# Wider parameter products, merged transposing loads, a dropped plane and moved stores in a backward pass of a state-space and SwiGLU block

## The chip, the cores and the metric

One NeuronCore of one Trainium2 chip runs the whole program in one launch. TensorE does the matrix products, VectorE and ScalarE the elementwise work, GpSimd a little elementwise work and one of the transfer queues; SyncE only issues transfers. SyncE, ScalarE and GpSimd each work through their own transfers in order, and an issue that must wait holds up what stands behind it on that engine. The metric is the device time of the launch in microseconds (us).

## What is computed

The forward pass, and then the gradients of its output with respect to twelve of its inputs. `L` is 2048 rows, `D` 576 channels, `N` 128 states per channel, `F` 4608 hidden units; everything comes in and goes out as bf16.

```python
xn  = layernorm(x)                                   # x is A_u
dt  = exp(log_dt);  A = A_re + 1j*A_im               # [D, N]
K   = einsum("dn,dnl,dn->dl", C, exp(dt*A*l), dt*B).real
s   = causal_conv(K, xn) + xn*Dskip                  # by FFT, length 2L
g   = silu((silu(xn @ w1) * (xn @ w3)) @ w2)
out = x + s*g
# returned: out and d<out, grad_out> / d(A_u, A_re, A_im, B_re, B_im, C_re, C_im,
#                                        log_dt, Dskip, w1, w3, w2)
```

So the backward pass needs, beside the gradients of the weights, the sum over the 2048 positions of the gradient of `K` against `exp(dt*A*l)`, for each channel and state, with and without a factor `l`: these sums are the "parameter sums" `S_all` below. With `l = a*64 + b` the exponential is split into a table over `b` (called Q, 64 values) and one over `a` (called P or PZ, `AV` = 32 values), each with a real and an imaginary plane.

## The kernel before, in words

The program is unrolled. Every piece of work has a due time, set by `self.at(us)`, and a planner orders each engine's instructions by these due times, by the dependencies between tiles and by its own costs; it also puts in all waits. The due times are planned microseconds, shorter than real ones. A tile pool gives out buffers by name; a name with one buffer is given to the next user only when the last reader of the former is done.

The stages in order of time:

1. Prologue, layer norm, and the spectra of `xn`.
2. `ssm_kernel` and `ffn_hidden`, interleaved. `kgen_chunk` makes the tables for 16 channels at a time (36 chunks): it multiplies magnitudes by sines and cosines into `q` and `pz`, stores them to `Q_dram` and `PZ_dram`, and uses them for the convolution kernel. `pz` has three planes, (-cos, sin, cos) times the magnitude; plane 0 is made from plane 2 by GpSimd (L477), and all three are stored (L478).
3. `forward_tail`: output of the feed-forward block, convolution, and the tiles that the backward pass keeps.
4. `backward`, groups. The hidden layer is worked through in 18 groups of 256 units (`phase6_group`). For a group, w2 is loaded transposed (`load_w2T`: two loads of 128 rows into `w2rows` on the GpSimd queue, two transposing loads on SyncE's queue); TensorE forms `ph` (L1226), ScalarE copies it to `gh` (L1229), VectorE multiplies it into the gradients of the two gates, `gg` and `gu` (L1232), which live in the tiles X and Y. Both are stored to `GG_dram` and `GU_dram` (L1239, two stores of 8 row tiles for each, on SyncE's queue, written behind the loop in the source) and used by TensorE for the gradients of w1 and w3 (`phase6_grad13`, L1273) and, with the hidden activation, of w2 (`phase6_grad2`, L1254). The GpSimd queue loads the next group's tiles from `GI_dram` (L1193, L1194).
5. Beside the groups run first the backward convolution (`ssm_bwd_conv`), then from its end on 19 parameter chunks (`param_chunk`); the other 17 run in stage 6.
6. `phase6_inputs`: the gradient with respect to `xn`, 16 row tiles. For each, `acts` loads `GG_dram` and `GU_dram` with a transposing load (tiles ggc and guc), TensorE multiplies them with the transposed w1 and w3 (L1333, 144 matmuls a tile, results in px or pgw), and VectorE and ScalarE finish the layer norm's backward pass (L1343, L1373 to L1384). The transposed w1 and w3 lie in four pairs of tiles: wTA (12 blocks of 128 hidden units each, loaded during the groups), wTB (12), a pair in the former goT buffers (4), and a pair in the former go_o buffer (8). Each is loaded by `wT_into` in five transposing loads, one for each 128 channels (the fifth has 64).

A parameter chunk (`param_chunk`) loads the gradient of K (gz, L978), the transposed Q table (qT, L1140) and pz (L983, two buffers). For each half of its 16 channels TensorE fills two PSUM tiles `et_ps` (three buffers) with 16 matmuls (L989); VectorE multiplies them with the planes of pz into `pr_q` (one buffer), two products of 512 elements a partition (L996), and sums over r and the 32 positions (L998), once for s = 0 and once for s = 1.

When the chunks of 128 channels are done, `final_block` turns their sums into gradients: TensorE transposes S_all, ScalarE copies (ST, L1026), VectorE works in two scratch tiles f0 and f1 (L1029 to L1076), ScalarE scales the results into `gout` (L1050) and issues their stores (L1051). There are five blocks, due after chunks 20, 30, 33 and twice 35.

All transposing loads go through `nat_transpose` (L1140) on SyncE's queue, so in the profile they share that line and are told apart by their tiles.

Of the kernel before, what the change touches and what calls it, by code (L numbers as in the profile page):

```python
# [16 lines left out]
P = 128  # L17
# [43 lines left out]
class K:  # L61
# [356 lines left out]
    def ssm_kernel(self, T0, TK):  # L418
# [10 lines left out]
        self.PZ_dram = self.dram.tile([P, NCH, 3, DC, AV], BF16, name="PZ_dram")  # L429
# [25 lines left out]
    def kgen_chunk(self, ch, E, lhs, mp, sb, qvp, ps, T, TK):  # L455
# [15 lines left out]
        pz = sb.tile([P, 3, DC, AV], BF16, name="pz_k")  # L471
        for k, src in ((1, S), (0, C)):
            tt(out=q[:, :, k, :], in0=E[:, 0:QW].rearrange("p (d b) -> p d b", b=BV),
               in1=src[:, 0:QW].rearrange("p (d b) -> p d b", b=BV), op=ALU.mult)
            tt(out=pz[:, 1 + k].rearrange("p d a -> p (d a)"), in0=E[:, QW:], in1=src[:, QW:], op=ALU.mult)
        nc.sync.dma_start(out=self.Q_dram[ch], in_=q[:].rearrange("p d k b -> p (d k b)"))
        nc.gpsimd.tensor_scalar(out=pz[:, 0], in0=pz[:, 2], scalar1=-1.0, scalar2=None, op0=ALU.mult)  # L477
        nc.sync.dma_start(out=self.PZ_dram[:, ch], in_=pz[:])  # L478
        v = qvp.tile([P, 2, DC, AV], BF16, name="v_k")
        for k, (Wa, Wb, op) in enumerate(((self.WrT, self.nWiT, ALU.add), (self.nWiT, self.WrT, ALU.subtract))):  # L480
            t = sb.tile([P, DC, AV], BF16, name="t_k")
            for r, W, o in ((1, Wb, t[:]), (0, Wa, v[:, k])):
                tt(out=o.rearrange("p d (a x) -> p d a x", x=4),
                   in0=pz[:, 1 + r].rearrange("p d (a x) -> p d a x", x=4),
# [246 lines left out]
    def forward_tail(self, T0, TB, TQ, gctx):  # L731
# [87 lines left out]
        self.w2rows = [rowp.tile([P, DT * P], BF16, name=f"w2r{i}") for i in range(4)]  # L819
        for w2r in self.w2rows:  # L820
            nc.gpsimd.memset(w2r[:, D:DT * P], 0.0)
# [41 lines left out]
    def ssm_bwd_params(self, chunk_at, final_at, out, big, S_all, ps):  # L863
# [4 lines left out]
        with self.tc.tile_pool(name="g_k", bufs=1, side="right") as gkp, self.tc.tile_pool(name="g_t", bufs=3, side="right") as tqp, \  # L868
                self.tc.tile_pool(name="g_q", bufs=2, side="right") as qp, \
                self.tc.tile_pool(name="g_r", bufs=1, side="right") as rp:  # L870
            gz = []
# [98 lines left out]
    def param_chunk(self, ch, gz, S_all, tqp, qp, rp, ps):  # L970
# [3 lines left out]
        if True:  # L974
# [8 lines left out]
            nc.sync.dma_start(out=pz[:], in_=self.PZ_dram[:, ch])  # L983
            for h in range(2):
                T = [ps.tile([P, 8, 2, AV], FP32, name="et_ps") for _ in range(2)]
                for dd in range(8):
                    dl = 2 * dd + h
                    for r in range(2):
                        nc.tensor.matmul(T[r][:, dd].rearrange("p k (f t) -> p (k f) t", f=2), lhsT=qT[:, dl, :],  # L989
                                         rhs=gK[:, r, :, :, dl, :].rearrange("p k f t -> p (k f) t"),  # L990
                                         start=True, stop=True)
                d0 = h * (D // 2) + ch * 8
                for s in range(2):
                    pr = rp.tile([P, 2, 8, 2, AV], FP32, name="pr_q")
                    for r in range(2):
                        nc.vector.tensor_tensor(out=pr[:, r], in0=T[r][:], in1=pz[:, s + r, h * 8:h * 8 + 8, :][:, :, None, :]  # L996
                                                .to_broadcast([P, 8, 2, AV]), op=ALU.mult)
                    nc.vector.tensor_reduce(out=S_all[:, 2 * s:2 * s + 2, d0:d0 + 8].rearrange("p k d -> p d k"),  # L998
                                            in_=pr[:].rearrange("p r d k a -> p d k r a"), op=ALU.add, axis=AX.XY)
# [10 lines left out]
    def final_block(self, c, do, dsz, fp, fo, S_all, ps2):  # L1010
# [18 lines left out]
        A, B = [fp.tile([P, 4, N], FP32, name=f"f{n}")[v] for n in range(2)]  # L1029
# [49 lines left out]
    def backward(self, T0, TG, TQ, TX, gctx, mats):  # L1079
# [11 lines left out]
        with ExitStack() as out:  # L1091
# [52 lines left out]
    def load_w2T(self, gi, T):  # L1144
# [66 lines left out]
    def phase6_group(self, gi, tiles, gwp, ps_h, ps_gw, defer):  # L1211
# [5 lines left out]
        for s in range(LH // 2):  # L1217
# [261 lines left out]
```

## Time and profile before

| | us |
|---|---|
| median of 5 runs | 2009.98 |
| lowest and highest | 2004.52, 2027.39 |
| the profiled execution, whole | 2007.47 |
| its span, first to last instruction | 2005.7 |

| engine | busy, us | share of the span | instructions |
|---|---|---|---|
| TensorE, matmuls | 1762.4 | 88% | 17108 |
| TensorE, weight loads | 1294.9 | 65% | 17179 |
| VectorE | 1420.5 | 71% | 2660 |
| ScalarE | 1024.0 | 51% | 1739 |
| GpSimd | 270.1 | 13% | 362 |

The mean granted TensorE clock is 0.961 of full speed. The transfers move 417.10 MB in 612,906 packets; SyncE's queue has 280.47 MB of it, GpSimd's 106.94 MB, ScalarE's 27.02 MB.

In the profile's names PE is TensorE, PEld its weight loads, DVE VectorE, ACT ScalarE, POOL GpSimd, SP SyncE; a name with a q behind it is that engine's queue of transfers. L996 is line 996 of the kernel. A line "A <- B: t" in a list of waits says that A's engine stood still for t us until B was done. Busy times of matmuls are modelled, since matmuls overlap, so TensorE can be "busy" at less than its peak. A DMA share of 1 means that the 16 DMA engines are taken all the time.

### The profile page before, as it was taken

The page shows a single profiled execution, that of the slowest core. Times are in us where ns is not written, and L with a number is a line of the kernel's source. Part 1 is how long each engine was busy: PE and PEld are TensorE (multiplying, and loading weights), DVE is VectorE, ACT ScalarE, POOL GpSimd, SP SyncE. Part 2 cuts the span into 40 slices and gives each one's busy share as a digit, 9 for nine tenths or more (in the row PEclk, how much of TensorE's full clock was granted, in tenths as well). Part 3 has the DMA queues.
Part 4 walks back from the last instruction along what each step waited for, and adds up shares of the span by engine and source line. Part 5 has one row for each costly group of instructions (what it writes and reads, how often), then busy time and mean ns, then how long its engine had stood idle before and what let it go on. Part 6 is the DMA issues. An engine that isn't in the chain of part 4 may idle for free. (4 is left out here: it accounts for less than half of the span.)

```text
span 2005.7 us, 41885 instructions
## 1 busy us (share of the span) xinstructions
PE 1762.4 (88%) x17108; PEld 1294.9 (65%) x17179; DVE 1420.5 (71%) x2660; ACT 1024.0 (51%) x1739; POOL 270.1 (13%) x362
## 2 busy tenths in 40 slices
PE   2789999999899988999989998879988967989888
PEld 1444444444488867777777777768777845767666
DVE  7538888888487743585984968758979913489786
ACT  2778888888555564764666656435445300100112
POOL 4003333333322121000000000100000000000000
PEclk9899999999899989999999999989999978989999
DMA  3589888797966597365563655798998999999992
GB/s 86 183 295 322 305 297 297 265 325 277 305 183 175 142 239 217 115 175 155 180 186 115 180 168 153 213 236 229 233 200 211 206 203 183 193 192 212 222 190 54
DMA packets 612906, 417.10 MB, mean 208 GB/s; under 512 B 400394, under 2 KB 558058, under 8 KB 607978
## 3 DMA queue, kind: packets, MB, share of 16 engines
q1 hardware_dynamic: 547200, 280.47, 56.9%
q0 software_dynamic: 24288, 106.94, 15.5%
q10 hardware_dynamic: 41226, 27.02, 5.1%
q8 instruction: 134, 2.20, 0.5%
q14 instruction: 58, 0.48, 0.1%
HBM read 134.06 MB, written 188.01 MB: 161 GB/s over the span
## 5 line engine op out<-in xcount | busy, mean ns | idle before, releaser
L719 PE MATMUL pgu<-wmB_w,xnT 128*128 128x512 bf16 x1088 | 273.4, 380 | 6.4 <-issue 3.2
L1273 PEld LDWEIGHTS <-xn_bf 128*128 128x128 bf16 x2304 | 223.9, 98 | 29.4 <-issue 2.7
L1273 PE MATMUL pgw<-Y,xn_bf 128*128 128x256 bf16 x2048 | 232.1, 273 | 1.7 <-ACT gw L1275 1.6
L996 DVE TENSOR_TENSOR pr_q<-et_ps,pz 128x512 f32<-128x512 f32 x288 | 186.3, 684 | 43.8 <-PE et_ps L989 35.9
L1226 PE MATMUL ph<-w2T,goT 128*128 128x256 bf16 x1440 | 193.1, 283 | 22.9 <-ACT gh L1229 22.7
L719 PEld LDWEIGHTS <-xnT 128*128 128x128 bf16 x1152 | 103.2, 98 | 124.1 <-issue 18.9
L998 DVE TENSOR_REDUCE S_all<-pr_q 128x16 f32<-128x1024 f32 x144 | 175.3, 1217 | 2.2
L1226 PEld LDWEIGHTS <-goT 128*128 128x128 bf16 x1440 | 142.1, 101 | 34.8 <-issue 13.7
L1232 DVE TENSOR_TENSOR Y<-gh,Y 128x1024 bf16<-128x1024 bf16 x128 | 86.6, 684 | 108.2 <-ACT gh L1229 106.6
L785 PE MATMUL po<-w2g,hc 128*128 128x288 bf16 x1152 | 154.4, 292 | 4.1 <-DMA hc<-H_dram 4.1
L1275 ACT CAST gw<-pgw 128x256 bf16<-128x256 f32 x144 | 54.0, 377 | 198.3 <-PE pgw L1273 198.3
L1333 PEld LDWEIGHTS <-ggc 128*128 128x128 bf16 x1152 | 114.7, 101 | 51.0 <-DMA wTB<-in_B_w_dram 11.1
L1333 PEld LDWEIGHTS <-guc 128*128 128x128 bf16 x1152 | 115.0, 101 | 46.9 <-DMA guc<-GU_dram 14.7
L785 PEld LDWEIGHTS <-hc 128*128 128x128 bf16 x1152 | 113.2, 100 | 34.4 <-DMA hc<-H_dram 4.5
L1373 ACT ACTIVATE X<-X 128x576 f32<-128x576 f32 x16 | 10.9, 683 | 223.2 <-DVE X L1343 223.2
L1254 PE MATMUL pgw<-go_o,X 128*128 128x288 bf16 x896 | 119.7, 287 | 0.0
L722 ACT ACTIVATE s_t<-pgu 128x512 bf16<-128x512 f32 x144 | 87.3, 609 | 51.9 <-PE pgu L721 51.6
L1229 ACT CAST gh<-ph 128x512 bf16<-128x512 f32 x144 | 84.1, 617 | 55.4 <-PE ph L1226 36.3
L1254 PEld LDWEIGHTS <-X 128*128 128x128 bf16 x960 | 93.3, 98 | 23.4 <-issue 0.6
L582 PEld LDWEIGHTS <-dSi 128*128 128x128 bf16 x768 | 75.5, 99 | 36.1 <-issue 35.4
L989 PE MATMUL et_ps<-gz,qT 128*128 128x64 bf16 x1152 | 57.3, 198 | 45.5 <-DVE pr_q L996 36.6
L989 PEld LDWEIGHTS <-qT 128*128 128x128 bf16 x1152 | 49.0, 101 | 74.2 <-DVE pr_q L996 33.3
(328 smaller groups left out, 4025.3 us busy)
## 6 DMA issues: line engine op xcount, KB each, us to landing
GI_dram<-gu_t POOLq DMA_DIRECT2D x72, 512.0 KB, 5.6
Y<-GI_dram POOLq DMA_DIRECT2D x19, 1024.0 KB, 6.9
H_dram<-h_t SPq DMA_DIRECT2D x72, 256.0 KB, 5.2
Q_dram<-q_k SPq DMA_DIRECT2D x36, 512.0 KB, 5.0
X<-GI_dram POOLq DMA_DIRECT2D x18, 1024.0 KB, 8.0
GU_dram<-Y SPq DMA_DIRECT2D x34, 512.0 KB, 5.3
GG_dram<-Y SPq DMA_DIRECT2D x30, 512.0 KB, 4.9
E_dram<-E_k SPq DMA_DIRECT2D x18, 768.0 KB, 3.7
```

The source lines that it names most:

```text
L719: nc.tensor.matmul(pgu[:, j], lhsT=xnT[:, c, ts], rhs=wm[w][:, c, :], start=(c == 0), stop=False)
L722: nc.scalar.activation(out=s_t[:, :, q, :], in_=pgu[:, 0].rearrange("p (g f) -> p g f", g=ng), func=ACT.Silu)
L785: nc.tensor.matmul(pos[k][:, pi_, 0:pw], lhsT=hcs[k][:, fi, :], rhs=w2[fi][:, po:po + pw], start=(fi == 0), stop=(fi == FT - 1))
L989: nc.tensor.matmul(T[r][:, dd].rearrange("p k (f t) -> p (k f) t", f=2), lhsT=qT[:, dl, :], rhs=gK[:, r, :, :, dl, :].rearrange("p k f t - ...
L996: nc.vector.tensor_tensor(out=pr[:, r], in0=T[r][:], in1=pz[:, s + r, h * 8:h * 8 + 8, :][:, :, None, :] .to_broadcast([P, 8, 2, AV]), op= ...
L998: nc.vector.tensor_reduce(out=S_all[:, 2 * s:2 * s + 2, d0:d0 + 8].rearrange("p k d -> p d k"), in_=pr[:].rearrange("p r d k a -> p d k r ...
L1226: nc.tensor.matmul(ph[j][:, k, :].rearrange("p (a f) -> p a f", f=P), lhsT=lw, rhs=rh, start=(n == 0), stop=(n == nfull))
L1229: nc.scalar.copy(out=gh[:, j], in_=ph[j])
L1232: nc.vector.tensor_tensor(out=t_[:, sl], in0=gh.rearrange("p j t f -> p (j t) f"), in1=t_[:, sl], op=ALU.mult)
L1254: nc.tensor.matmul(pgw[pi_][:, 0:pw], lhsT=hn[:, tt, fl * P:(fl + 1) * P], rhs=go_o[:, tt, po:po + pw], start=(tt == 0), stop=(tt == LT - 1))
L1273: nc.tensor.matmul(pw_[:, 0:FG], lhsT=self.xn_bf[:, tt, c * P:(c + 1) * P], rhs=nat[:, tt, :], start=(tt == 0), stop=(tt == LT - 1))
L1333: nc.tensor.matmul(px[pi_][:, 0:pw], lhsT=act[:, fi, :], rhs=wT[ai][fi][:, po:po + pw], start=(fi == 0 and ai == 0), stop=(fi == FT - 1 an ...
```

## The change

Four edits, and what they drag along.

- Products: the PSUM tile's order changes from (channel, k, position) to (k, channel, position). One product now covers both values of s, with the PSUM operand repeated: two products of 1024 elements and one sum over 2048 elements for a half chunk, in place of four products of 512 and two sums over 1024. `pr_q` becomes twice as large. The scratch A and B of `final_block` no longer is f0 and f1 but lies in a buffer of the name pr_q, of which there is one.
- Weights: `wT_into` loads all 576 channels with one transposing load, so 8 loads in place of 40; wTA's two loads are due at T2 - 90 and T2 - 54, where the ten were due from T2 - 160 to T2 - 52 (T2 is the planned end of the groups). `load_w2T` loads its 256 rows with one load and one transposing load.
- The plane: `PZ_dram` holds (sin, cos) only. GpSimd's negation is gone; `param_chunk` loads two planes and ScalarE makes the third (-cos) in each of the 36 chunks.
- Stores: the GG and GU stores are issued on GpSimd's queue, in the source behind the second and the fourth quarter of a group's loop.

```diff
@@ ssm_kernel, kgen_chunk
-        self.PZ_dram = self.dram.tile([P, NCH, 3, DC, AV], BF16, name="PZ_dram")
+        self.PZ_dram = self.dram.tile([P, NCH, 2, DC, AV], BF16, name="PZ_dram")
...
-        pz = sb.tile([P, 3, DC, AV], BF16, name="pz_k")
+        pz = sb.tile([P, 2, DC, AV], BF16, name="pz_k")
...
-            tt(out=pz[:, 1 + k].rearrange("p d a -> p (d a)"), in0=E[:, QW:], in1=src[:, QW:], op=ALU.mult)
+            tt(out=pz[:, k].rearrange("p d a -> p (d a)"), in0=E[:, QW:], in1=src[:, QW:], op=ALU.mult)
...
-        nc.gpsimd.tensor_scalar(out=pz[:, 0], in0=pz[:, 2], scalar1=-1.0, scalar2=None, op0=ALU.mult)
@@ forward_tail
-        self.w2rows = [rowp.tile([P, DT * P], BF16, name=f"w2r{i}") for i in range(4)]
+        self.w2rows = [rowp.tile([P, self.FG // P, DT * P], BF16, name=f"w2r{i}") for i in range(2)]
@@ param_chunk
-            nc.sync.dma_start(out=pz[:], in_=self.PZ_dram[:, ch])
+            nc.sync.dma_start(out=pz[:, 1:3], in_=self.PZ_dram[:, ch])
+            nc.scalar.activation(out=pz[:, 0], in_=pz[:, 2], func=ACT.Copy, scale=-1.0)
             for h in range(2):
-                T = [ps.tile([P, 8, 2, AV], FP32, name="et_ps") for _ in range(2)]
+                T = [ps.tile([P, 2, 8, AV], FP32, name="et_ps") for _ in range(2)]
                 for dd in range(8):
                     dl = 2 * dd + h
                     for r in range(2):
-                        nc.tensor.matmul(T[r][:, dd].rearrange("p k (f t) -> p (k f) t", f=2), lhsT=qT[:, dl, :],
-                                         rhs=gK[:, r, :, :, dl, :].rearrange("p k f t -> p (k f) t"),
+                        nc.tensor.matmul(T[r][:, :, dd].rearrange("p k (f t) -> p k f t", f=2), lhsT=qT[:, dl, :],
+                                         rhs=gK[:, r, :, :, dl, :],
                                          start=True, stop=True)
                 d0 = h * (D // 2) + ch * 8
-                for s in range(2):
-                    pr = rp.tile([P, 2, 8, 2, AV], FP32, name="pr_q")
-                    for r in range(2):
-                        nc.vector.tensor_tensor(out=pr[:, r], in0=T[r][:], in1=pz[:, s + r, h * 8:h * 8 + 8, :][:, :, None, :]
-                                                .to_broadcast([P, 8, 2, AV]), op=ALU.mult)
-                    nc.vector.tensor_reduce(out=S_all[:, 2 * s:2 * s + 2, d0:d0 + 8].rearrange("p k d -> p d k"),
-                                            in_=pr[:].rearrange("p r d k a -> p d k r a"), op=ALU.add, axis=AX.XY)
+                pr = rp.tile([P, 2, 4, 8, AV], FP32, name="pr_q")
+                for r in range(2):
+                    nc.vector.tensor_tensor(out=pr[:, r].rearrange("p (s k) d a -> p s k (d a)", s=2),
+                                            in0=T[r][:].rearrange("p k d a -> p k (d a)")[:, None]
+                                            .to_broadcast([P, 2, 2, 8 * AV]),
+                                            in1=pz[:, r:r + 2, h * 8:h * 8 + 8, :].rearrange("p s d a -> p s (d a)")
+                                            [:, :, None, :].to_broadcast([P, 2, 2, 8 * AV]), op=ALU.mult)
+                nc.vector.tensor_reduce(out=S_all[:, :, d0:d0 + 8], in_=pr[:].rearrange("p r k d a -> p k d r a"),
+                                        op=ALU.add, axis=AX.XY)
@@ final_block
-        A, B = [fp.tile([P, 4, N], FP32, name=f"f{n}")[v] for n in range(2)]
+        ws = self.rp.tile([P, 2, 4, 8, cfg.AV], FP32, name="pr_q")[v].rearrange("p r k d a -> p (r k d a)")
+        A, B = [ws[:, n * 4 * N:(n + 1) * 4 * N].rearrange("p (k n) -> p k n", n=N) for n in range(2)]
@@ backward
-                self.wT_into(t[:], ai, 0, wT, lambda c: T2 - 160 + 12 * (2 * c + ai))
+                self.wT_into(t[:], ai, 0, wT, T2 - 90 + 36 * ai)
@@ wT_into
-        for c, (do, dsz) in enumerate(self.cfg.dch):
-            self.at(at(c))
-            self.nat_transpose(dst[:, :, do:do + dsz], self.aps[("B_w1", "B_w3")[ai]][do:do + dsz, f0 * P:(f0 + n) * P])
+        self.at(at)
+        self.nat_transpose(dst, self.aps[("B_w1", "B_w3")[ai]][:, f0 * P:(f0 + n) * P])
@@ load_w2T
-        for fl in range(nfl):
-            fi = gi * nfl + fl
-            w2r = self.w2rows[fi % len(self.w2rows)]
-            nc.gpsimd.dma_start(out=w2r[:, 0:cfg.D], in_=self.aps["B_w2"][fi * P:(fi + 1) * P, :])
-            self.nat_transpose(w2T[:, fl], w2r[:])
+        w2r = self.w2rows[gi % len(self.w2rows)]
+        nc.gpsimd.dma_start(out=w2r[:, :, 0:cfg.D], in_=self.aps["B_w2"][gi * self.FG:(gi + 1) * self.FG, :].rearrange(
+            "(l p) d -> p l d", p=P))
+        self.nat_transpose(w2T[:].rearrange("p l c f -> p (l c) f"), w2r[:].rearrange("p l d -> p (l d)"))
@@ phase6_group
+            if s % 2 == 1:
+                ts = slice(s // 2 * LH, (s // 2 + 1) * LH)
+                for (dst, t_) in ((self.GU_dram, gu), (self.GG_dram, gg)):
+                    nc.gpsimd.dma_start(out=dst[ts, :, gi * FG:(gi + 1) * FG].rearrange("t p f -> p t f"),
+                                        in_=t_[:, ts, :])
             if s % 2 == 1 and not defer:
                 self.phase6_grad2(gi, s // 2, hn, ps_gw, "pgw")
-        for (dst, t_) in ((self.GU_dram, gu), (self.GG_dram, gg)):
-            for j in range(2):
-                ts = slice(j * LH, (j + 1) * LH)
-                nc.sync.dma_start(out=dst[ts, :, gi * FG:(gi + 1) * FG].rearrange("t p f -> p t f"), in_=t_[:, ts, :])
         self.phase6_grad13(gi, gg, gu, gwp, ps_gw)
```

More of the change, by code (lines that the diff above doesn't have):

```diff
@@ L483, in kgen_chunk @@
                 tt(out=o.rearrange("p d (a x) -> p d a x", x=4),
-                   in0=pz[:, 1 + r].rearrange("p d (a x) -> p d a x", x=4),
+                   in0=pz[:, r].rearrange("p d (a x) -> p d a x", x=4),
                    in1=W[:, ch].rearrange("p h d x -> p (h d) x")[:, :, None, :].to_broadcast([P, DC, AV // 4, 4]),
@@ L818, in forward_tail @@
             nc.gpsimd.memset(t_[rem:P, nfull, :], 0.0)
-        self.w2rows = [rowp.tile([P, DT * P], BF16, name=f"w2r{i}") for i in range(4)]
+        self.w2rows = [rowp.tile([P, self.FG // P, DT * P], BF16, name=f"w2r{i}") for i in range(2)]
         for w2r in self.w2rows:
-            nc.gpsimd.memset(w2r[:, D:DT * P], 0.0)
+            nc.gpsimd.memset(w2r[:, :, D:DT * P], 0.0)
         out0 = aps["out_0"].flatten_outer_dims()
@@ L870, in ssm_bwd_params @@
                 self.tc.tile_pool(name="g_r", bufs=1, side="right") as rp:
+            self.rp = rp
             gz = []
@@ L1307, in weights @@
                 for ai in range(2):
-                    self.wT_into(tiles[ai], ai, f0, wT, lambda c: t)
+                    self.wT_into(tiles[ai], ai, f0, wT, t)
                 return f0 + tiles[0].shape[1]
```

## The prediction

> **What bounds the kernel now.** I read the table by stage, then the waits of each engine, then the timelines of SyncE's queue, VectorE and ScalarE around the waits that TensorE pays for. From 100 to 785 us (kernel generation, hidden layer, forward tail) TensorE is 87 to 98% busy; the change touches that part only at the edges. Two later stages matter: the groups (785 to 1600, where from 1290 on parameter chunks run in between) and the input gradient (1600 to the end, with the other 17 chunks). The first two columns of the next view are the stretch and its length, then the busy time of TensorE, its weight loads, VectorE, ScalarE, GpSimd, then the TensorE clock, DMA share and GB/s:
>
> ```profile
> 1285.00:1600.00 315.00, 279.43 (x2949) 237.38 (x2949) 255.77 (x357) 137.70 (x228) 17.49 (x28) 0.95 0.94 219
> ...
> 1625.00:1636.00 11.00, 1.13 (x19) 0.88 (x16) 0.00 (x0) 0.00 (x0) 0.00 (x0) 0.68 1.14 200
> ...
> 1745.00:1975.00 230.00, 198.50 (x1866) 152.62 (x1864) 191.03 (x337) 26.12 (x61) 9.55 (x18) 0.93 1.03 196
> ```
>
> From 1745 on VectorE (83%), TensorE (86%) and the DMA engines (1.03) are all near full; the chain of waits runs there through VectorE's pr_q and S_all. Where a weight load is late, TensorE stands still. Who made TensorE and ScalarE wait, in the chunk part of the groups and after 1600 (sum, times, longest):
>
> ```profile
> PE ph L1226 <- ACT gh L1229: 16.4, 3, 11.2
> PE et_ps L989 <- DVE pr_q L996: 12.9, 11, 8.4
> ```
> ```profile
> ACT gh L1229 <- DMA wTA<-in_B_w_dram: 13.9, 1, 13.9
> ```
> ```profile
> PE px L1333 <- DMA wTB<-in_B_w_dram: 11.0, 1, 11.0
> ```
>
> The first and third are one event: seven wTA pieces fill SyncE's queue from 1323.1 to 1343.6, ScalarE holds a store behind one of them, its gh copies stand behind the store, and TensorE waits 11.2 us. SyncE's queue at the start of the last stage:
>
> ```profile
> 1614.20 21.53 SPq L1140 DMA_TRANSPOSE wTB<-in_B_w_dram  x10
> ...
> 1647.74 14.14 SPq L1140 DMA_TRANSPOSE go_o<-in_B_w_dram  x10
> ```
>
> and the two rows of the parameter products:
>
> ```profile
> L996 DVE TENSOR_TENSOR pr_q<-et_ps,pz 128x512 f32<-128x512 f32 x288 | 186.3, 684 | 43.8 <-PE et_ps L989 35.9 <-DMA pz<-PZ_dram 3.9 <-DVE S_all L998 0.5
> L998 DVE TENSOR_REDUCE S_all<-pr_q 128x16 f32<-128x1024 f32 x144 | 175.3, 1217 | 2.2
> ```
>
> **Products.** A chunk now costs VectorE 8 x 0.684 + 4 x 1.217 = 10.34 us. Between the rows, 512 elements more cost 0.533 us, 1.04 ns each. A product over 1024 elements I therefore put at 1.217, a sum over 2048 at 1.217 + 1.067 = 2.28: 4 x 1.217 + 2 x 2.28 = 9.43. That is 0.91 us less a chunk, 33 us over 36. What lies on the path: between 1745 and 1975 there are 60 sums, 15 chunks, so 13.7 us, taken whole because VectorE leads the chain there; TensorE at 198.5 of 230 is next, so more than 30 us can't come. In the groups VectorE is at 81% and TensorE paid 12.9 us for it. PSUM tiles now come free after one product instead of three: I take half, 6. (Bounds 0 and 12.9.) TensorE's 32 matmuls a chunk keep their size and only write in another order: nothing.
>
> The final blocks' scratch now is the one pr_q buffer. So the first product after a block waits until ScalarE's last gout copy has read it, and behind that product stand the next chunk's and, by PSUM, TensorE's et_ps matmuls. Today the next block's first f product waits in that place: four times, 29.7 us, because a gout store hangs behind a guc transfer on ScalarE's queue. The wait thus moves rather than appears, but the products that now run between block and wait (1747.9 to 1753.0, four products and two sums) no longer do: about 5 us for each of three blocks with chunks after them, 15 at most, 0 if ScalarE is not held. I take +6.
>
> **Weights.** Four tile pairs lose 8 of 10 loads each; the bytes stay. wTB and go_o, 3.54 and 2.36 MB, take 35.7 us of queue, 165 GB/s. The ggc and guc loads between them, 4.72 MB in 25.3 us, run at 187; the last ggc and guc alone, 1950.1 to 1959.4, 2.36 MB in 9.2 us, at 256. So the merged loads save 4 us (31.6) to 12.6 (23.1). A load of 576 rows is nowhere in the trace and the first matmuls now wait for a whole tile instead of its first rows, so it may also lose up to 5 us. I take -9, near the undisturbed row: little but these loads runs there, and the DMA strip shows gaps between the ten go_o pieces. TensorE follows one to one: wTB ends its 11.0 us wait, and go_o, landing by 1664, sets the end of tile 0 at 1667.5, on whose buffer the next ggc load at 1667.62 waits. The wTA event (11.2 us): two loads 36 planned us apart replace ten; I take -8, as one 1.77 MB load (7 us at 256 GB/s) can still hold a ScalarE store. w2T: 36 loads at 1.23 us become 18 of twice the size; nobody waits for them but the GpSimd queue, which is idle: 0.
>
> The Trainium skill, in Advanced Engine Details and Errata, section X-Bar Transpose (TRN2), puts transposing DMAs at 350 to 400 GB/s. No row here reaches that (256 at best); by its lower figure 5.9 MB would take 16.9 us, the saving be 19, and the whole sum 10 us lower.
>
> **The plane of p.** GpSimd's 36 negations (1.544 us each, 55.6 us) lie in a stage where it is 30% busy (118.5 of 400 us): nothing. Reading 128 KB less a chunk is 0.5 us of DMA at 256 GB/s; DMA is full at the end: -2 in all. The price is 36 negations on ScalarE of 128x512, nearest the gh copy (0.617 us): 22 us, on an engine that is 44% busy in the chunk part of the groups and 11% later. Worse is the wait: the negation stands in ScalarE's order and waits for the pz load (4.0 us to landing), and behind it stand gh copies, gw copies and stores. In the groups SyncE issued pz 3 to 10 us late in five of 19 chunks (4.1, 3.0, 5.4, 9.7, 3.3: 25 us). The first product comes 7 us or more after that issue (chunk 0 aside), so where the order puts the negation late it costs nothing. TensorE got 11.2 of 13.9 us of ScalarE's one long wait. Bounds 0 and 25 x 0.8 = 20 plus landings; I take +7.
>
> **Stores.** 72 GG/GU stores leave SyncE's queue, where they took 0.4 to 0.9 us each and held it 50.5 us behind L1232. On GpSimd's queue they stand before and after w2r, X and Y loads; that engine is 4 to 6% busy, and a store like GI_dram cost it 0.954. The next gg load waits for the TensorE tail L1281 at 1534.75, the store before it was issued 14 us earlier: a store passes in time. TensorE waited for no store. Bounds -10 (a freer SyncE brings qT and pz earlier) and +10 (a load behind a store that waits for L1232); I take -2. To landing, the SyncE stores took 5.3 us and GpSimd's GI_dram 5.6: no difference. The skill's DMA: Bandwidth & Descriptors, section Issuing engines are not separate DMA queues, speaks against this part: another queue saves only issuing time; by it the part is worth 0 and the sum 2 us higher.
>
> **Sum.** -13.7 - 6 + 6 - 9 - 8 + 7 - 2 - 2 = -27.7. The profiled execution took 2007.47 (span 2005.7 and 1.8 around it), so 1979.8; the median of the runs is 2.5 above it: 1982.
>
> **Rivals.**
> Small gain: the merged loads run no faster (DMA share is 1.10 to 1.14 from 1614 to 1636, which speaks for it; the gaps in the go_o stretch against), and the blocks give the product gain back: -4 for wTB and go_o, -4 for wTA, -13.7 - 6 + 15 = -4.7 for the products, +7 - 2 - 2 for the rest: -10, 2000.
> Slower: the negation holds ScalarE for pz in every chunk of the groups. Each us of wait costs 19 x 0.8 = 15 us; against the 35 us of the other terms it decides from 2.3 us a chunk. At landing time (4.0) it gives +61 - 35 = +26, at 3.5 +18: 2028. For it: ScalarE waits 22.4 us for Y loads already. Against: in most chunks need lags issue by 7 to 20 us.
> Large gain: both late stages fall to TensorE's pace. A tile's 144 matmuls run in 17.6 us where nothing waits (pairs 0.245 us apart at 1654), 19 with a chunk's 32 beside them, but the last 14 tiles took 316 us, 22.6 each. Half of the difference over 14 tiles is -25 more: 1957.
>
> **Numbers.** Forecast 0.50 (1965 to 1995), small gain 0.18, slower 0.20, large gain 0.12. About 1% is what a measurement can tell from no change. Faster: 0.47 + 0.12 = 0.59; within: 0.03 + 0.18 + 0.02 = 0.23; slower 0.18. The range, 1948 to 2028, leaves out half of the large gain's low side and of the slow case.
>
> **What would show it.** Products at 1.2 and sums at 2.3 us; L989's wait for pr_q under 25 us in all; wTB and go_o pairs under 28 us of SyncE's queue; no 11 us wait of L1226; ScalarE's wait for pz, absent today, under 1 us a chunk. I am wrong if that wait is above 2, or if the wait for gout before a product passes 15 us a block.

## The result, and the profile after

| | before | after |
|---|---|---|
| median of the runs beside each other, us | 2015.46 (79 runs) | 2036.42 (44 runs) |
| lowest and highest | 1993.63, 2043.06 | 2015.20, 2064.74 |
| the profiled execution, whole and span | 2007.47, 2005.7 | 2033.11, 2031.3 |

The ratio is 1.0101, with an interval of 1.0082 to 1.0119: the change made the kernel one per cent slower. 1982 was forecast, and the time lies above the range. The ratios here and below compare the runs within 1.5% of the fastest of the same kernel; in e1 below these are four of twelve, and the median of all its twelve, 2008.60 us, is that of the kernel before beside it, 2008.70. In the profiled executions the difference of the spans is +25.6 us. By the starts of TensorE's matmuls it falls into four pieces: up to the first `ph` of the groups (781.1 and 796.1, +14.9), first to last `ph` (797.1 and 827.1, +30.0), from there to the first `px` of the last stage (39.2 and 43.1, +3.9), and from there to the end (388.2 and 365.1, -23.1). So what was meant for the last stage arrived there, and the groups lost more than that.

First the page of the changed kernel, the costliest groups of instructions (lines have moved: L1001 is the sum that was L998, and L984 is the new negation):

```profile
L996 DVE TENSOR_TENSOR pr_q<-et_ps,pz 128x1024 f32<-128x1024 f32 x144 | 170.6, 1218 | 138.7 <-PE et_ps L990 112.4
...
L1001 DVE TENSOR_REDUCE S_all<-pr_q 128x32 f32<-128x2048 f32 x72 | 164.3, 2283 | 1.0
...
L984 ACT ACTIVATE pz<-pz 128x512 bf16<-128x512 bf16 x36 | 22.7, 631 | 259.6 <-DMA pz<-PZ_dram 243.9
```

Products and sums cost what the row arithmetic said (1.218 and 2.283 us). But VectorE now waits 112.4 us for TensorE's `et_ps`, where it was 35.9 (81.1 with the products alone, run e7 below), and 36 negations that take 22.7 us have 259.6 us of ScalarE's idle time in front of them. Who made whom wait, over the whole span of the changed kernel (sum, times, longest):

```profile
ACT pz L984 <- DMA pz<-PZ_dram: 243.9, 28, 39.5
...
PE pgw L1276 <- ACT gw L1278: 29.6, 8, 9.8
...
DVE pr_q L996 <- ACT gout L1054: 15.4, 2, 9.2
...
PE ph L1228 <- ACT gh L1231: 13.0, 11, 1.9
```

and, of the kernel before,

```profile
PE pgw L1273 <- ACT gw L1275: 1.6, 3, 0.8
```

TensorE's wait for `gw`, 1.6 us before, is 29.6. The 11.2 us wait for `gh` is gone (longest 1.9), and the first product behind a final block waits at most 9.2 us for `gout`. ScalarE's wait for pz was to be under 1 us a chunk, and above 2 was to mean that I am wrong: it is 80.7 us in the 20 chunks up to 1640 us, 4 a chunk. SyncE's queue at the start of the last stage, two pairs that were ten loads each, 21.53 and 14.14 us, before:

```profile
1664.45 14.60 SPq L1143 DMA_TRANSPOSE wTB<-in_B_w_dram  x2
...
1691.20 9.75 SPq L1143 DMA_TRANSPOSE go_o<-in_B_w_dram  x2
```

One wait close up, in the groups: lines from the timelines of SyncE, ScalarE, TensorE and GpSimd between 1497 and 1519 us (start, duration, engine, line; in brackets the idle time before and what ended it):

```profile
1497.90 4.12 SPq L1143 DMA_TRANSPOSE qT<-Q_dram  x1
1502.12 2.90 SPq L1143 DMA_TRANSPOSE w2T<-w2r  x1
1505.13 0.54 SPq L983 DMA_DIRECT2D pz<-PZ_dram  x1
```
```profile
1517.06 0.63 ACT L984 ACTIVATE pz<-pz 128x512 bf16<-128x512 bf16 x1 [12.88 <-DMA pz<-PZ_dram]
1517.59 0.63 ACT L1278 CAST gw<-pgw 128x256 bf16<-128x256 f32 x2
```
```profile
1507.16 1.03 PE L1276 MATMUL pgw<-Y,xn_bf 128*128 128x256 bf16 x8 [0.34 <-DVE Y L1234]
1518.00 1.22 PE L1276 MATMUL pgw<-Y,xn_bf 128*128 128x256 bf16 x5 [9.80 <-ACT gw L1278]
```
```profile
1504.26 0.57 POOL L1196 DMA_DIRECT2D X<-GI_dram  x1 [4.42 <-PE pgw L1257]
1507.42 0.90 POOL L1239 DMA_DIRECT2D GU_dram<-Y  x1 [2.60 <-DVE Y L1234]
1508.31 0.89 POOL L1239 DMA_DIRECT2D GG_dram<-Y  x1
```

Read from the bottom: an X load of 1 MB and two stores of 0.5 MB start within 4 us of a pz load of 0.25 MB, which takes 12 us to land and was itself issued 0.1 us after the w2T load ahead of it on SyncE's queue. ScalarE stands before the negation of chunk 12 for 12.88 us. The `gw` copies behind it are of matmuls that ended at 1508.2; TensorE stands 9.80 us for their PSUM buffers. The products of chunk 12 need the negated plane only at 1543.2, 26 us after it was made: nobody needed it then.

### The profile page after: what moved, and what is told of

Its sections match the earlier page's. It is cut to its first block, busy times and chain, and to the rows that moved or that the text cites. A ratio compares the mean times of both kernels' runs of the same rounds, so it can differ in the third digit from the quotient of the medians.

```text
span 2031.3 us, 41504 instructions
## 1 busy us (share of the span) xinstructions
PE 1762.2 (87%) x17108; PEld 1298.7 (64%) x17179; DVE 1397.3 (69%) x2444; ACT 1042.1 (51%) x1775; POOL 271.2 (13%) x378
## 5 line engine op out<-in xcount | busy, mean ns | idle before, releaser
L1276 PEld LDWEIGHTS <-xn_bf 128*128 128x128 bf16 x2304 | 228.9, 100 | 65.7 <-issue 34.3
L1276 PE MATMUL pgw<-Y,xn_bf 128*128 128x256 bf16 x2048 | 241.6, 279 | 31.1 <-ACT gw L1278 29.6
L996 DVE TENSOR_TENSOR pr_q<-et_ps,pz 128x1024 f32<-128x1024 f32 x144 | 170.6, 1218 | 138.7 <-PE et_ps L990 112.4
L1228 PE MATMUL ph<-w2T,goT 128*128 128x256 bf16 x1440 | 183.7, 275 | 13.0 <-ACT gh L1231 13.0
L1001 DVE TENSOR_REDUCE S_all<-pr_q 128x32 f32<-128x2048 f32 x72 | 164.3, 2283 | 1.0
L1228 PEld LDWEIGHTS <-goT 128*128 128x128 bf16 x1440 | 137.7, 98 | 32.2 <-issue 14.9
L984 ACT ACTIVATE pz<-pz 128x512 bf16<-128x512 bf16 x36 | 22.7, 631 | 259.6 <-DMA pz<-PZ_dram 243.9
L727 POOL DMA_DIRECT2D GI_dram<-gu_t x72 | 66.5, 924 | 369.1 <-DVE gu_t L723 218.5
L1257 PEld LDWEIGHTS <-X 128*128 128x128 bf16 x960 | 92.3, 98 | 22.7 <-issue 0.5
L723 ACT CAST gu_t<-pgu 128x1024 bf16<-128x1024 f32 x90 | 92.0, 1022 | 22.0 <-DMA GI_dram<-gu_t 22.0
L1231 ACT CAST gh<-ph 128x512 bf16<-128x512 f32 x144 | 83.6, 617 | 36.0 <-PE ph L1228 34.4
```

The source lines that it names most:

```text
L723: cp(out=gu_t[:, :, :, q, :], in_=pgu[:].rearrange("p u (g f) -> p u g f", g=ng))
L996: nc.vector.tensor_tensor(out=pr[:, r].rearrange("p (s k) d a -> p s k (d a)", s=2), in0=T[r][:].rearrange("p k d a -> p k (d a)")[:, None ...
L1001: nc.vector.tensor_reduce(out=S_all[:, :, d0:d0 + 8], in_=pr[:].rearrange("p r k d a -> p k d r a"), op=ALU.add, axis=AX.XY)
L1228: nc.tensor.matmul(ph[j][:, k, :].rearrange("p (a f) -> p a f", f=P), lhsT=lw, rhs=rh, start=(n == 0), stop=(n == nfull))
L1231: nc.scalar.copy(out=gh[:, j], in_=ph[j])
L1257: nc.tensor.matmul(pgw[pi_][:, 0:pw], lhsT=hn[:, tt, fl * P:(fl + 1) * P], rhs=go_o[:, tt, po:po + pw], start=(tt == 0), stop=(tt == LT - 1))
```

## The experiments

All runs are over five rounds beside the kernel before. The stage columns are from one profiled execution each, by the same matmuls as above: groups, first to last `ph` (797.1 before, 827.1 after), and rest, from there to the end (427.5 before, 408.2 after). With one profile each, ten us of a column say little: e9, whose ratio is 0.9988, has 9.4 us less in the groups than the kernel before. Plane, products, weights, stores are the four parts of the change.

| run | kernel | ratio to before, interval | groups | rest |
|---|---|---|---|---|
| e1 | changed, plane undone | 0.9878 (0.9825 to 0.9931) | 786.1 | 406.0 |
| e2 | before + plane | 1.0127 (1.0072 to 1.0182) | 821.2 | 413.1 |
| e3 | changed, negation on VectorE | 1.0107 (1.0061 to 1.0152) | 824.0 | 414.1 |
| e4 | changed, pz load ahead of gz | 1.0063 (1.0021 to 1.0104) | 830.2 | 407.5 |
| e5 | changed, sign in the product | 0.9859 (0.9814 to 0.9904) | 786.7 | 404.1 |
| e6 | changed, negation later | 0.9976 (0.9929 to 1.0022) | 800.5 | 407.0 |
| e7 | before + products | 0.9876 (0.9841 to 0.9911) | 783.2 | 414.5 |
| e8 | before + weights | 0.9928 (0.9896 to 0.9960) | 791.0 | 411.5 |
| e9 | before + stores | 0.9988 (0.9954 to 1.0022) | 787.7 | 428.2 |
| e10 | before + products + weights | 0.9835 (0.9797 to 0.9873) | 780.7 | 404.8 |
| e11 | e5, stores back on SyncE | 0.9839 (0.9795 to 0.9883) | 783.2 | 400.7 |
| e12 | changed, stores back on SyncE | 0.9940 (0.9902 to 0.9977) | 809.8 | 398.5 |
| e13 | changed, stores on GpSimd, old place | 1.0078 (1.0039 to 1.0116) | 823.3 | 403.3 |
| e14 | changed, wTA in pieces | 1.0135 (1.0088 to 1.0181) | 833.8 | 410.9 |
| e15 | e11, wTA in pieces | 0.9806 (0.9769 to 0.9842) | 778.0 | 392.5 |
| e16 | before + products, later weight pairs merged | 0.9856 (0.9812 to 0.9900) | 790.6 | 408.3 |

**The plane, taken out and put in alone.** e1 gives the changed kernel its three stored planes back, e2 gives the kernel before two and the negation. The part of e1's edit in `param_chunk` (the three planes and GpSimd's negation in `kgen_chunk` come back with it):

```diff
-            nc.sync.dma_start(out=pz[:, 1:3], in_=self.PZ_dram[:, ch])
-            nc.scalar.activation(out=pz[:, 0], in_=pz[:, 2], func=ACT.Copy, scale=-1.0)
+            nc.sync.dma_start(out=pz[:], in_=self.PZ_dram[:, ch])
```

> The changed kernel with three planes of p stored again and the negation back on GpSimd in kernel generation; products, weight loads and stores stay as changed. Theory N (the ScalarE negation stands in ScalarE's order and waits for the pz load, which stands behind the gz loads on SyncE's queue; gw and gh copies stand behind it, TensorE behind them): the 244 us of ScalarE's wait for pz go to 0, TensorE's wait for gw falls from 29.6 back to under 5 us, and the time is 0.98 to 0.99 of the kernel before (some 1975 to 1995). Rival S (the stores on GpSimd's queue cost the time): still 1.00 to 1.02. Rival F (the 15 us lost in the forward tail at 520 to 560 us, not the negation, are most of it, whatever their cause): 1.00, with the groups no faster than in the changed kernel.

> The kernel before with the plane part alone: two planes of p stored, the third made by ScalarE in each parameter chunk. Theory N: slower than before by 25 to 50 us, 1.012 to 1.025, ScalarE waiting over 150 us in all for pz, TensorE over 15 us for gw. Rival S (the stores): within 0.5% of before, ScalarE's wait for pz may be there but TensorE doesn't pay for it. Rival F: slower only by the 15 us of the forward tail, 1.007, and the groups as long as before (772 us from the first ph matmul to the last group's start).

e1's ratio is 0.9878, e2's 1.0127. e1's is the weakest of the study, since its twelve runs spread from 1969.43 to 2017.54 us; e5 below (0.9859), whose six lie between 1972.08 and 1994.03, says the same of the changed kernel without the negation. In e1 TensorE's wait for `gw` is back at 1.4 us; in e2 it is 33.4, with ScalarE waiting 241.5 us for pz:

```profile
ACT pz L983 <- DMA pz<-PZ_dram: 241.5, 28, 48.3
...
PE pgw L1273 <- ACT gw L1275: 33.4, 9, 8.1
```

The plane part is the cause, beside the other parts and without them; it is the groups that pay for it (+41.0 us between e1 and the changed kernel, +24.1 between before and e2).

**Who holds the negation, and what the load waits for.** e3 writes `nc.vector.tensor_scalar(...)` for the ScalarE instruction. e4 issues the load first:

```diff
+            pz = qp.tile([P, 3, 16, AV], BF16, name="pz")
+            nc.sync.dma_start(out=pz[:, 1:3], in_=self.PZ_dram[:, ch])
+            nc.scalar.activation(out=pz[:, 0], in_=pz[:, 2], func=ACT.Copy, scale=-1.0)
             for k in range(2):
                 nc.sync.dma_start(out=gK[64 * k:64 * k + 64, 1 - k].rearrange("p k f d t -> p (k f d t)"),
                                   in_=self.gK_dram[g, :, cc].rearrange("p k f d -> p (k f d)"))
...
-            pz = qp.tile([P, 3, 16, AV], BF16, name="pz")
-            nc.sync.dma_start(out=pz[:, 1:3], in_=self.PZ_dram[:, ch])
-            nc.scalar.activation(out=pz[:, 0], in_=pz[:, 2], func=ACT.Copy, scale=-1.0)
```

> The changed kernel with the negation of pz on VectorE in place of ScalarE, nothing else. VectorE would wait for pz before the products anyway. Theory N: ScalarE is free of pz; VectorE pays 36 x 0.3 to 0.7 us, 11 to 25 us, of which the 17 chunks of the last stage lie on its path (5 to 12 us): 0.985 to 0.995 of before. Rival S: 1.01 or more. A third, V: a negation at the head of VectorE's order holds the gh products as it held ScalarE's copies, so nothing is regained: 1.01.

> The changed kernel with the pz load and its negation issued ahead of the two gz loads on SyncE's queue, nothing else. If the loop is what costs (gz load waits for TensorE's et_ps matmuls, pz stands behind gz, ScalarE waits for pz, TensorE for ScalarE), pz comes as soon as its own buffer is free: ScalarE's wait for pz falls from 244 us to under 60, TensorE's wait for gw from 29.6 to under 10, the time to 0.985 to 0.995 of before. If the wait for pz comes from its own buffer (two of them, freed by VectorE's products of two chunks ago) or from the transfer itself, the wait stays over 150 us and the time at 1.01.

Both fell against my theory of that time, that ScalarE alone is held and that the gz loads delay pz. VectorE is held just as ScalarE was, the case called V. Its waits in e3:

```profile
DVE pz L984 <- DMA pz<-PZ_dram: 128.2, 19, 24.8
...
PE et_ps L990 <- DVE pr_q L996: 57.7, 23, 13.3
```

In e4 the wait is 211.0 us and the groups as long as in the changed kernel (its profiled execution, 2043.32 us, is the second longest of its twelve, whose median is 2024.33), so the gz loads of the same chunk aren't what delays pz. The issue times say more. In the changed kernel, of the 17 chunks from 2 to 18, nine have their pz load issued within 0.3 us of the end of VectorE's products of chunk c-2, which frees its buffer: 1360.8 after 1360.7, 1402.3 after 1402.2, 1447.5 after 1447.5. (The same count, nine of 17, can be read in the trace of before.) But ScalarE hardly waits in those nine, 8.1 us in all. In the other eight the buffer has been free for 0.7 to 6.6 us and the pz load follows 0.1 to 0.2 us behind the load ahead of it on SyncE's queue, qT, w2T or goT, and there ScalarE waits 49.4 us. In e2 the two sums are 9.4 us in ten chunks and 51.7 in seven. So most of the wait stands where pz is held up by SyncE's queue. What would shorten it, a third pz buffer or another queue for pz, no run has tried. The load lands 3 to 12 us after its issue, and the negation stands in its engine's order right there, from chunk 2 on 10 to 37 us before the chunk's first product.

**No negation, or a later one.** In e5 two planes are loaded and VectorE applies the sign:

```diff
-            nc.scalar.activation(out=pz[:, 0], in_=pz[:, 2], func=ACT.Copy, scale=-1.0)
...
+                nc.vector.scalar_tensor_tensor(out=o0[0], in0=Tf[0], scalar=-1.0, in1=b1(1), op0=ALU.mult, op1=ALU.mult)
+                nc.vector.tensor_tensor(out=o0[1], in0=Tf[0], in1=b1(0), op=ALU.mult)
```

In e6 ScalarE's factor is a column that VectorE makes from the sums of the chunk before:

```diff
+                nc.vector.tensor_scalar(out=m1[:], in0=S_all[:, 0, ch * 8 - 8:ch * 8 - 7], scalar1=0.0, scalar2=-1.0,
+                                        op0=ALU.mult, op1=ALU.add)
-            nc.scalar.activation(out=pz[:, 0], in_=pz[:, 2], func=ACT.Copy, scale=-1.0)
+            nc.scalar.activation(out=pz[:, 0], in_=pz[:, 2], func=ACT.Copy, scale=m1)
```

> The changed kernel without a negated plane at all: two planes of p are loaded, and the product with -C is written by VectorE as (T x -1) x C; the wide product of r = 0 is cut into two of 512 elements for it. In the three slower kernels the pz load of chunk c was issued the moment the products of chunk c-2 ended, and the negation stood in some engine's order right behind its landing, 15 to 25 us before the products need it. Theory N', the instruction that waits for pz early is the whole cost: with none, the time is that of the version with the plane undone plus 4 to 7 us for the cut product (15 chunks on the path x 2 x 0.15, and a part in the groups): 0.988 to 0.993 of before, no wait over 5 us of TensorE for gw. Rival T, the smaller planes or the later pz issue cost in themselves (DMA order, other plan): still over 1.00.

> The changed kernel with the same ScalarE negation, but its factor -1 is read from a column that VectorE writes out of the sums of the chunk before (36 instructions of one element per partition more), so that in the plan and on the chip the negation of chunk c comes behind the sums of chunk c-1 instead of behind the landing of its pz. Theory N': ScalarE's wait for the pz load falls from 244 us to under 40, TensorE's wait for gw from 29.6 to under 8, the time to 0.985 to 0.995. If ScalarE now waits as long for VectorE's sums, or the products for the negation (over 40 us in all), the place in the order isn't free to choose and the time stays at 1.00 to 1.015.

e5 keeps the smaller planes and loses nothing: 0.9859, its groups as long as with the plane undone. So it isn't the planes, it is the instruction that waits. The expectation set the price of the sign too high: the product with the sign costs what a plain one of its size does, 0.686 us beside 0.681. e6 met its first case in the waits (ScalarE's for pz 36.3 us, TensorE's for `gw` 1.4) and missed it in the time: ScalarE now waits 115.7 us for VectorE's column, as the second case had it. Its groups lie between, 800.5, and its interval holds 1.

**The other parts alone.** The edits are the hunks of the change themselves.

> The kernel before with the wide products, sums and the final blocks' scratch in pr_q alone. By the prediction's terms -13.7 - 6 + 6 = -14 us: 0.990 to 0.996; VectorE's products and sums 335 us in place of 361. If the final blocks give the gain back, 0.998 to 1.003, with VectorE's wait for gout before a product over 15 us a block.

> The kernel before with one transposing load per weight tile alone (wTA, wTB, go_o, w2T). By the prediction's terms -9 - 8 = -17 us: 0.989 to 0.995, the 11.2 us wait of TensorE behind the wTA store gone and the wTB and go_o pairs under 28 us of SyncE's queue. If the loads only run as fast as before: 0.996 to 1.002.

> The kernel before with the GU and GG stores alone moved, issued on GpSimd's queue after each half of a group. By the prediction's term -2 us, bounds -10 and +10: 0.995 to 1.005. Products alone gave 0.9876 and weights alone 0.9928, 0.981 together, but with the stores (and without the plane part) it is 0.9878: if the stores give something back, 1.003 to 1.010 here; if products and weights overlap in what they save, 0.998 to 1.002 here.

> The changed kernel without the plane part and without the moved stores: products and weights alone. If their gains add, 0.978 to 0.983 (some 1970 us); if they overlap, 0.985 to 0.989 as with the stores.

Products are worth more than forecast (0.9876; 13.9 us in the groups and 13.0 in the rest of its profile), weights about as much as forecast (0.9928), the stores nothing that can be told (0.9988, the interval holds 1). Products and weights nearly add. In e8 the wait that the merged wTA load was to end is still there, 11.6 us: the second wTA load holds SyncE's queue for 23.20 us, and ScalarE waits 15.58 us for a Y load that runs at the same time.

**The stores beside the negation.** e11 and e12 put the stores back on SyncE's queue in e5 and in the changed kernel; e13 leaves them on GpSimd's but in their old place (the same lines with `nc.gpsimd`):

```diff
-            if s % 2 == 1:
-                ts = slice(s // 2 * LH, (s // 2 + 1) * LH)
-                for (dst, t_) in ((self.GU_dram, gu), (self.GG_dram, gg)):
-                    nc.gpsimd.dma_start(out=dst[ts, :, gi * FG:(gi + 1) * FG].rearrange("t p f -> p t f"),
-                                        in_=t_[:, ts, :])
...
+        for (dst, t_) in ((self.GU_dram, gu), (self.GG_dram, gg)):
+            for j in range(2):
+                ts = slice(j * LH, (j + 1) * LH)
+                nc.sync.dma_start(out=dst[ts, :, gi * FG:(gi + 1) * FG].rearrange("t p f -> p t f"), in_=t_[:, ts, :])
```

> The version with the sign in the product (two planes of p, no negation) and the stores back on SyncE's queue. If the stores cost 3 to 10 us in that setting, 0.978 to 0.984; if they cost nothing, 0.984 to 0.988; if SyncE's queue with 72 stores again delays qT and pz, 0.988 or more.

> The changed kernel, ScalarE's negation and all, with the stores back on SyncE's queue and in their old place. The plane part costs 25 us alone (1.0127) but some 45 us on top of the three others (1.0101 against 0.9878). If the stores on GpSimd's queue make the negation's wait worse, 0.997 to 1.003 and a ScalarE wait for pz well under 244 us; if they have no part in it, 1.005 to 1.013 and the wait as long.

> The changed kernel with the GU and GG stores still issued by GpSimd, but in their old place behind the group's last half instead of after each half. With the stores back on SyncE the changed kernel fell from 1.0101 to 0.994. If it is GpSimd's queue (X and Y loads and the gz clearing behind stores that wait for VectorE, and stores and X loads in flight together with the pz load that ScalarE waits for) that makes the negation dearer, 1.005 to 1.012 here too; if it is the earlier place in the order, 0.992 to 0.998.

Without a negation the stores' queue makes no difference that can be told (0.9859 and 0.9839). With it, it is worth 1.6%: 1.0101 falls to 0.9940, more than either case of e12 said. e13 is at 1.0078, its interval apart from e12's, so it is the queue and not the place. TensorE's waits in the chunk part of the groups, in the changed kernel (1275 to 1623 us) and in e12 (1262 to 1592):

```profile
PE pgw L1276 <- ACT gw L1278: 28.2, 6, 9.8
PE et_ps L990 <- issue: 13.1, 1, 13.1
PE pgw L1282 <- ACT gw L1278: 6.2, 2, 5.1
PE ph L1228 <- ACT gh L1231: 4.4, 4, 1.7
```
```profile
PE ph L1228 <- ACT gh L1231: 14.4, 4, 12.4
PE pgw L1275 <- ACT gw L1277: 8.0, 4, 4.2
PE pgw L1281 <- ACT gw L1277: 6.9, 3, 3.3
PE et_ps L990 <- DMA gz<-gK_dram: 4.6, 1, 4.6
```

The waits for `gw` are 34.4 us against 14.9, the wait before the first chunk 13.1 against 4.6 (that one is there without a negation too, see the next paragraph), and the `gh` waits go the other way, 4.4 against 14.4. All waits of TensorE in these windows sum to 58.1 and 39.7, a difference of 18.4 beside groups that differ by 17.3. One cause that can be read is the landing: over 15 chunks (3 to 16 and 18) ScalarE's negation starts 5.7 us after the issue of pz in the changed kernel and 4.3 in e12, at most 11.9 and 7.5. That stores and X loads on one queue, in flight together, make it so is argued from the close-up above, and was not isolated; in e2, with the stores on SyncE's queue, the same mean is 6.0 and the longest 12.0, so the landing doesn't follow from the stores' queue alone.

**The merged wTA loads.** In the changed kernel SyncE's queue holds two wTA loads ahead of the first chunk's:

```profile
1309.76 11.26 SPq L1143 DMA_TRANSPOSE wTA<-in_B_w_dram  x1
1321.20 1.13 SPq L978 DMA_DIRECT2D gz<-gK_dram  x2
1322.38 4.85 SPq L1143 DMA_TRANSPOSE qT<-Q_dram  x1
```

and TensorE's 13.1 us, the second line of the waits above, are spent at 1332 before that chunk's first matmul. e14 and e15 load wTA in pieces again, e16 (with plane and stores as before) w2T as well:

```diff
-                self.wT_into(t[:], ai, 0, wT, T2 - 90 + 36 * ai)
+                for c, (do, dsz) in enumerate(cfg.dch):
+                    self.at(T2 - 160 + 12 * (2 * c + ai))
+                    self.nat_transpose(t[:, :, do:do + dsz], self.aps[("B_w1", "B_w3")[ai]][do:do + dsz, 0:FA * P])
+                for f in range(FA):
+                    wT[ai][f] = t[:, f, :]
```

> The changed kernel with the two wTA tiles loaded in five pieces each again, at the old times. In the changed kernel two wTA loads of 7.1 and 11.3 us stand on SyncE's queue ahead of the first chunk's gz and qT loads, and TensorE stands 13.1 us before the first chunk. If that is what the one load per wTA tile costs, this wait goes and the time falls by 8 to 13 us, 1.003 to 1.007; if the pieces bring the 11 us wait behind ScalarE's store back, 1.007 to 1.012.

> The version with the sign in the product and the stores on SyncE's queue (0.9839), with wTA in pieces at the old times. If the one load per wTA tile costs in the groups what it saves, 0.982 to 0.986; if it is a loss there, 0.976 to 0.981; if a gain, 0.987 or more.

> The kernel before with the wide products and, of the loads, wTB and go_o alone merged; wTA and w2T, the plane and the stores as before. By the stages of the runs so far products give 14 us in the groups and 13 after them, wTB and go_o about 10 after them: 0.979 to 0.984. If w2T's merging or wTA's is a part of the 0.9835 of products and weights together, 0.985 to 0.988.

e14 missed both cases. The wait before the first chunk falls from 13.1 to 5.6 us, but TensorE's waits for `gw` grow from 34.4 to 50.2 us, and the groups are no shorter: beside the negation one removed wait is taken back by another.

The 13.1 us are not the merged loads' alone. In the seven profiled kernels with merged wTA loads and the stores on GpSimd's queue, both wTA loads stand ahead of the first chunk's gz and qT, and TensorE waits 13.1 to 23.6 us before that chunk (6.0 in e4). In the four with merged wTA loads and the stores on SyncE's queue (e8, e10, e11, e12) the second wTA load comes behind the first chunk's, and the wait is 4.6 to 5.1, as it is with wTA in pieces (4.7 to 6.9). The negation has no part in it: e5 waits 20.6 us, e11 5.1.

e15, without the negation and with the stores on SyncE's queue, has the lowest ratio of the study, 1967.41 us (median of 6) beside 2006.29. Its interval overlaps e11's, so whether the pieces or the single load are better is not settled; e16 (0.9856) doesn't settle it either.

## Why the prediction was wrong

**The step that failed** is the plane's: "so where the order puts the negation late it costs nothing", and with it "Bounds 0 and 25 x 0.8 = 20 plus landings; I take +7". The order puts it early, from chunk 2 to 18 of the groups 10 to 37 us before the first product, so every late load holds ScalarE. That the planner places it where it expects pz to have landed is argued from this order; e6, which makes it wait for something later, takes about half of the loss away (0.9976, between 1.0101 and e5's 0.9859). That SyncE issues pz late in some chunks I had read rightly (25 us in five chunks; ScalarE then waited 49.4 us in eight), but I asked how long the products could wait for pz, and not where an instruction that waits for nothing but pz would stand. The landing, too, which counts where the negation stands right behind it, was in the bounds only as a word. Measured by single profiles, the plane costs +24.1 us in the groups alone (e2), +29.1 beside products and weights (e12 against e10), +41.0 beside the stores too (the changed kernel against e1).

**The slower rival** named the mechanism, "the negation holds ScalarE for pz in every chunk of the groups", and had 0.20. Its wait came out at 4 us a chunk (80.7 us over the 20 chunks before 1640 us), for which it gave +26; the profiled spans differ by +25.6. But that agreement is partly chance. Its price of 15 us for each us of wait is 0.8 of the wait; the runs give 24.1 of 69.1 us in e2, 29.1 of 46.3 in e12 and 41.0 of 80.7 in the changed kernel, 0.35 to 0.63. And 14.9 of the 25.6 us are lost before the groups, which neither case had priced (last section).

**The other terms.** From the last `ph` to the end the terms were -13.7 + 6 - 9 - 2 = -18.7; measured -19.3 in the changed kernel. Part by part it fits less well, so some of that is luck: -13.0 in e7, where -7.7 was taken, -16.0 in e8 for -9, and -22.7 with both (e10). For the groups the products' -6 was too small by half: e7 gives -13.9, in one profile. The -8 for the wTA event was right in name only: the 11 us wait is gone in the changed kernel, but the merged loads are not what ended it. TensorE's longest wait for `gh` is 1.9 to 3.8 us in all nine profiled kernels with the stores on GpSimd's queue, e9 and e14 with wTA in pieces among them, and 5.2 to 12.4 in the four with merged wTA loads and the stores on SyncE's queue (11.6 in e8). In the changed kernel the 13.1 us before the first chunk stand in its place. What the blocks' scratch costs by itself no run shows: VectorE's wait for `gout` before a product is 15.4 us in two waits, none above 9.2, where its wait before the next block's f was 29.7. wTB and go_o took 24.35 us of queue, within the bounds of 23.1 and 31.6 and 2.3 below the value taken.

The Trainium skill's Advanced Engine Details and Errata, section X-Bar Transpose (TRN2), puts such loads at 350 to 400 GB/s; wTB (3.54 MB in 14.60 us) and go_o (2.36 in 9.75) both ran at 242 here; the fastest merged loads in any run were a wTA tile of 1.77 MB in 6.76 us (e1), 262, and half of the go_o pair, 1.18 MB, in 4.32 us (e4), 273. So the row of 256 decided rightly.

**The stores.** -2 forecast, 0.9988 alone. The Trainium skill's DMA: Bandwidth & Descriptors, section Issuing engines are not separate DMA queues, which spoke against a gain, agrees with that. What I did not see is that beside the negation their move costs 1.6% (0.9940 to 1.0101): the term was costed against the kernel before, where ScalarE has no wait for pz.

Without the plane the sum was -27.7 - 7 + 2 = -32.7; e1's 1.2% is some 25 us of 2010, with the weakness of its runs said above, and e5's 1.4% some 28.

## What to carry to other kernels

An elementwise step that was moved next to a load stood right behind the load's landing here, and not just before its result was needed; there it held everything behind it for as long as the load was late, on ScalarE and on VectorE alike. Before pricing such a step, read from the trace when the loaded buffer comes free (here the end of the products two uses earlier) and what stands ahead of the load on its queue, and look for a form without a waiting step of its own: the sign inside an operation that has to wait anyway cost nothing that could be told. Price parts of a change together where they share a resource: stores that cost nothing alone cost 1.6% beside an engine that waited for loads, and with them on the other queue the merged wTA loads came ahead of the first chunk's.

## What the runs showed of the hardware

The stretch before the groups took from 779.5 to 803.8 us in the profiled executions. The same order of work does not make it the same: the changed kernel and e5 have the same order of ScalarE's instructions up to 1333 us and start the groups at 796.1 and 779.5. A relation to the kernel isn't excluded, though: the seven with three stored planes lie at 781.0 to 788.2, of the eleven with two planes eight at 790.9 or more and three (e2, e5, e12) at 779.5 to 782.0. One place where it happens is the start of the forward tail, in stretches of 5 us (length, busy time of TensorE, its weight loads, VectorE, ScalarE, GpSimd, then clock, DMA share, GB/s), the changed kernel and then e5:

```profile
520.00:525.00 5.00, 5.00 (x25) 1.86 (x25) 2.57 (x4) 2.39 (x4) 3.87 (x5) 1.00 1.32 154
525.00:530.00 5.00, 4.95 (x24) 1.89 (x24) 2.05 (x3) 2.40 (x4) 0.00 (x0) 1.00 1.30 44
530.00:535.00 5.00, 1.13 (x6) 0.38 (x5) 0.00 (x0) 0.00 (x0) 0.00 (x0) 1.00 1.25 53
```
```profile
520.00:525.00 5.00, 5.00 (x25) 1.89 (x23) 2.11 (x3) 2.79 (x5) 4.00 (x6) 1.00 1.20 321
525.00:530.00 5.00, 5.00 (x25) 1.79 (x22) 1.92 (x2) 1.77 (x3) 1.68 (x2) 1.00 1.02 364
530.00:535.00 5.00, 0.50 (x3) 0.19 (x3) 0.00 (x0) 0.00 (x0) 2.13 (x5) 0.98 1.05 405
```

In the first the DMA engines are as busy and move 44 to 53 GB/s instead of 364 to 405, for 10 us, and TensorE stands until 554.1 instead of 538.0. Why is open.

A transposing load of one 1.77 MB wTA tile held SyncE's queue between 6.76 us (262 GB/s, e1) and 23.20 us (76 GB/s, e8), the second beside a Y load and other traffic.
